# First score block in one plain fp32 pass, and what is rearranged around it

## Chip, cores, metric

The program runs on 1 core of a Trainium2 chip. The metric is device time in microseconds (us), the median of the runs. Lower is better.

## What is computed

Three parts follow each other: causal attention (2 batches, 12 heads, 448 positions, 64 per head), a token- and channel-mixing block, and a Fourier block with a normalized feed-forward network. Cut to the part that the change touches:

```python
scores = scale * np.matmul(q, k.transpose(0, 1, 3, 2))      # scale = 1 / 8
scores = np.where(mask, -1000000000.0, scores)              # mask: column > row
attn = np.exp(scores - np.max(scores, axis=-1, keepdims=True))
attn = attn / (np.sum(attn, axis=-1, keepdims=True) + 1e-09)
return np.matmul(attn, v)
```

Behind it stand `relu(xt @ w_tok1) @ w_tok2`, `relu(u @ w_ch1) @ w_ch2`, two Fourier transforms, and a feed-forward network with 3072 hidden channels.

## The kernel before

**Precision.** Products that must be exact to fp32 are split: an operand x becomes a rounded part "high" and a remainder "low", both of type fp32r, and the product is three fp32r passes: high x high, high x low, low x high. A plain fp32 matmul also exists in the kernel; the trace records each of those as two LDWEIGHTS and two MATMUL records. Transposes are single records.

**Pairs.** Attention goes by pairs of heads: 12 pairs (6 per batch). A pair's q and k lie as 128 x 448 tiles (64 rows for each head). `load_k` (K) loads k and q into staging slots, `k_high` (k) and `q_high` (q) round them on ScalarE (ACT), `k_low` (l, on GpSimd/POOL except for pair 0) and `q_low` (m, on VectorE/DVE) make the remainders. The four 112-row blocks of a pair's causal scores are made by `scores` (S) in three groups: S n.0 holds blocks 0 and 1, S n.1 block 2, S n.2 block 3. Block i needs 112 (i + 1) columns, but each pass has at least 256 columns (L336): `w = max(256, TS * (i + 1))`. The causal mask is added by bf16 matmuls (L354). Then follow the maxima (N, DVE), exps (E, ACT), transposes (T, L391, TensorE), their copies (C, DVE and ACT), the product with v (P, L408) and its copy (O, L416, ACT), the transposes of that (X, L427), the divisors (Z, L420) and the division (x, L440, DVE).

**Staging slots.** The loads of q and k use tiles that later hold the residual (they appear as `resid` in the trace). `stage(n)` (L290 to L292) hands them out in turn: six slots for pairs 0 to 4, three of them for pairs 5 to 11. A load into a slot waits until all readers of what was there are done. The order in which k and q of a pair take their slots is set in L297:

```python
c.k32, c.q32 = stage(n), stage(n)
nc.sync.dma_start(out=c.k32, in_=qk[b, hp, :, 1])
nc.sync.dma_start(out=c.q32, in_=qk[b, hp, :, 0])
```

So, from pair 6 on, k of pair n + 1 goes into the slot that q of pair n - 1 had, and q of pair n + 1 into that of k of pair n. All loads (q and k, v at L321, weights at L132) are issued by one queue, SP, in order.

**Order.** Every engine executes in the order of the program, and in the attention stage this order is written out by hand in the string `ORDER`: a letter, the pair and a part. The letters are those above, and R, W for loading and converting weights ahead (L132, L141 to L161), A, r, s, D, d for token mixing, B, b for channel layout, u, w for rounding the residual, h, g for rounding x. Within ORDER, `m8` (q_low of pair 8) stands behind `K9`, and `q10 u0.2 k10 R4 W4.0 N9.1 E9.0 O7 X7` is one stretch of line 84.

**Opening.** Before the attention stage TensorE executes seven 128 x 128 plain fp32 matmuls of a constant tile `mean_w` (L194), which VectorE has set (L117). POOL builds the identity and mask tiles (L267 to L276).

Of the kernel before, what the change touches and what calls it, by code (L numbers as in the profile page):

```python
# [10 lines left out]
F32 = mybir.dt.float32  # L11
# [59 lines left out]
ORDER = """K0 k0 l0 K1 q0 m0 S0.0 N0.0 N0.1 S0.1 N0.2 S0.2 k1 l1 N0.3 q1 m1 E0.0 E0.1 S1.0 N1.0 N1.1 K2 E0.2 S1.1 E0.3 T0.2 T0.0
N1.2 C0.2 k2 q2 E1.0 T0.1 T0.3 C0.0 T0.4 E1.1 l2 m2 S1.2 E1.2 S2.0 N1.3 V1 V0 C0.3 N2.0 C0.4 C0.1 P0 R0 W0.0 W0.1 N2.1
K3 K4 E1.3 k3 T1.0 T1.2 S2.1 T1.1 C1.0 O0 T1.4 T1.3 C1.2 X0 E2.0 q3 E2.1 N2.2 E2.2 S2.2 l3 m3 S3.0 C1.1 k4 Z0 x0 N2.3
C1.3 q4 C1.4 P1 N3.0 E2.3 T2.0 T2.3 T2.4 N3.1 S3.1 R1 W1.0 O1 T2.2 W0.2 m4 C2.0 B0.0 C2.3 T2.1 C2.4 X1 E3.0 E3.1 S3.2
N3.2 E3.2 l4 S4.0 V3 V2 b0.0 C2.1 C2.2 P2 W0.3 W0.4 W0.5 N3.3 N4.0 Z1 x1 N4.1 K5 q5 E3.3 T3.0 C3.0 T3.1 T3.2 Z2 O2
T3.4 k5 C3.2 C3.1 B0.1 X2 T3.3 E4.0 E4.1 S4.1 S4.2 C3.4 W1.1 b0.1 h0 C3.3 P3 l5 g0 N4.2 N4.3 E4.2 m5 S5.0 E4.3 S5.1 x2
T4.3 Z4 W1.2 Z3 T4.4 C4.4 O3 h1 T4.1 h2 T4.0 C4.3 T4.2 C4.0 C4.2 N5.0 X3 K6 C4.1 k6 N5.2 N5.1 B0.2 g2 g1 R2 W2.0 q6
A0.1 A0.0 x3 V5 V4 W1.3 W2.1 E5.0 E5.1 S5.2 l6 m6 E5.2 S6.0 W1.4 K7 r0.0 N5.3 P4 E5.3 S6.1 N6.0 N6.1 s0.0 r0.1 b0.2
T5.4 O4 k7 s0.1 X4 T5.1 T5.0 C5.4 T5.2 E6.0 E6.1 x4 W1.5 D0.0 C5.1 D0.1 N6.2 C5.0 T5.3 W2.2 S6.2 E6.2 q7 h3 l7 m7 S7.0
d0.1 C5.2 K8 q8 C5.3 P5 N6.3 R3 k8 h4 N7.0 E6.3 N7.1 d0.0 T6.4 T6.2 T6.0 E7.0 E7.1 S7.1 S7.2 O5 T6.3 l8 g4 V6 K9 C6.3  # L80
k9 C6.2 C6.4 B1.1 X5 C6.0 T6.1 D0.2 N7.2 m8 q9 Z5 x5 N7.3 W2.3 b1.1 B1.2 C6.1 B1.0 P6 Z6 d0.2 E7.2 S8.0 N8.0 N8.1 h5
E7.3 T7.3 O6 b1.2 T7.0 b1.0 T7.2 C7.3 T7.4 T7.1 C7.0 X6 E8.0 E8.1 S8.1 S8.2 C7.1 W2.4 Z7 g5 g3 C7.2 A1.1 C7.4 A1.0 x6
N8.2 B2.0 N8.3 W3.0 W3.1 W3.2 E8.2 l9 m9 S9.0 E8.3 S9.1 V7 P7 V8 K10 r1.1 s1.1 u0.1 h6 W2.5 Z8 u0.0 r1.0 s1.0 N9.0
T8.0 W3.3 T8.1 b2.0 T8.3 q10 u0.2 k10 R4 W4.0 N9.1 E9.0 O7 X7 C8.1 C8.0 T8.4 E9.1 C8.3 D1.0 x7 B2.1 T8.2 N9.2 S9.2 m10
E9.2 l10 w0.1 S10.0 C8.4 d1.0 C8.2 P8 b2.1 N9.3 E9.3 T9.2 T9.1 D1.1 W3.4 O8 h7 K11 q11 T9.0 W4.1 N10.0 N10.1 W4.2 C9.2
T9.3 C9.1 T9.4 E10.0 C9.3 E10.1 d1.1 X8 C9.0 D1.2 S10.1 S10.2 m11 x8 h8 k11 C9.4 V9 P9 V11 Z9 u1.0 N10.2 E10.2 N10.3
E10.3 d1.2 O9 W3.5 l11 S11.0 S11.1 B2.2 R5 W5.0 b2.2 T10.1 C10.1 T10.0 T10.2 g7 g8 w0.2 w0.0 g6 N11.0 N11.2 N11.1
T10.3 C10.3 u1.2 E11.0 A2.0 r2.0 C10.2 C10.0 X9 T10.4 W4.3 A2.1 W5.1 x9 W5.2 W4.4 E11.1 S11.2 s2.0 V10 C10.4 P10 N11.3
u1.1 E11.2 r2.1 s2.1 E11.3 T11.2 C11.2 T11.0 C11.0 T11.1 O10 T11.4 T11.3 W5.3 C11.4 X10 W4.5 R6 W6.0 W6.1 Z10 R7 C11.1
C11.3 P11 w1.2 D2.0 O11 X11 x10 D2.2 d2.2 Z11 x11 h10 d2.0 B3.1 b3.1 u2.0 h9 W5.4 w1.1 w1.0 U0 g10 B3.2 U1 W6.2 u2.2  # L90
y0 b3.2 h11 B3.0 y1 W5.5 W7.0 W7.1 W6.3 W6.4 g9 g11 A3.0 A3.1 z0 D2.1 b3.0 r3.0 s3.0 W7.2 z1 W7.3 r3.1 s3.1 U2 y2 D3.0
D3.1 d3.0 z2 d3.1 W7.4 U3 D3.2 y3 u3.1 W6.5 W7.5 w2.2 w2.0 d2.1 u3.0 u2.1 w3.0 w3.1 w2.1 z3 Y0 a0 d3.2 Y1 a1 u3.2 w3.2
"""


# [5 lines left out]
def fused_kernel(ctx: ExitStack, tc: tile.TileContext, qk, v, w1, w2, wa, wb, wc, wd, fa, fb, out):  # L101
    nc = tc.nc
# [12 lines left out]
    make_identity(nc, ident)  # L115
    mean_w = const.tile([128, 128], F32, name="mean_w")
    vec.memset(mean_w, 1.0 / DM)  # L117
    ones = const.tile([1, 128], F32, name="ones")
    vec.memset(ones, 1.0)
    eps_t = const.tile([128, 16], F32, name="eps_t")[:, :1]  # L120
    vec.memset(eps_t, EPS)
# [68 lines left out]

    ps = ctx.enter_context(tc.tile_pool(name="ps", bufs=1, space=bass.MemoryType.PSUM))
    psum = ps.tile([128, 8, 512], F32, name="psum")
    for _ in range(7):
        mm(psum[:, 7, :128], lhsT=mean_w, rhs=mean_w, start=True, stop=True)  # L194
    turn = dict(y=0, s=0, all=0)

    def take(ring, n):
# [63 lines left out]
    with ExitStack() as actx:  # L261
# [28 lines left out]
        def stage(n):  # L290
            staged[0] += 1
            return resid[staged[0] % 6 if n < 5 else 3 + staged[0] % 3][1]  # L292

        def load_k(n):
            c = pairs[n]
            b, hp = n // 6, n % 6
            c.k32, c.q32 = stage(n), stage(n)  # L297
            nc.sync.dma_start(out=c.k32, in_=qk[b, hp, :, 1])
            nc.sync.dma_start(out=c.q32, in_=qk[b, hp, :, 0])

# [709 lines left out]
```

## Time and profile before

| | |
|---|---|
| median of 3 runs | 685.57 us (685.55 to 686.62) |
| profiled execution, span from first to last instruction | 687.0 us |
| TensorE (PE) busy | 680.4 us, 99% |
| VectorE (DVE) busy | 534.8 us, 78% |
| ScalarE (ACT) busy | 291.7 us, 42% |
| GpSimd (POOL) busy | 125.5 us, 18% |
| q and k loads | 24, 224 KB each, 3.2 us from issue to landing (median) |

The profiled execution is one run more; its own time is the span. A busy share is an average over stages: the attention stage takes the first 125 us, in which ACT and DVE are busier than on average. TensorE's records overlap and their ends are modelled, so the distance between starts is what a matmul costs. An idle time in brackets at the end of a timeline row is what the engine stood still before that row, with what released it.

### The profile page before, as it was taken

What the parts mean: (1) busy time and instruction counts of PE and PEld (TensorE: products, weight loads), DVE (VectorE), ACT (ScalarE), POOL (GpSimd) and SP (SyncE); (2) the same over time, 40 slices, a digit from 0 to 9 for tenths busy, and PEclk for the clock granted to TensorE, in tenths of its full rate; (3) what the DMA queues carried; (4) which work ended last, traced back from release to release, by engine and by line L of the source; (5) the groups of instructions that cost most, each with busy time, mean ns of one, the idle gap of its engine ahead of it and who ended that gap; (6) DMA issues with size and microseconds to landing.
All of it is one profiled execution on the core that took longest, in us unless ns stands there. A gap on an engine that the chain in (4) does not pass through costs nothing.

```text
span 687.0 us, 10288 instructions
## 1 busy us (share of the span) xinstructions
PE 680.4 (99%) x3946; PEld 623.8 (91%) x3946; DVE 534.8 (78%) x885; ACT 291.7 (42%) x624; POOL 125.5 (18%) x106
## 2 busy tenths in 40 slices
PE   8999999999999999999999999999999999999997
PEld 7778888999999999999999999999999999999997
DVE  5997887367987975799989987989887898655851
ACT  6988987433333323244455522223443233323200
POOL 3153327420000000130140004372003221000000
PEclk9999999999999999999999999999999999999999
DMA  8234221164344342200223342324232434222311
GB/s 268 68 103 138 91 99 45 49 234 151 125 127 133 111 149 95 93 1 1 92 77 108 123 144 76 120 92 153 93 122 93 155 124 151 93 84 83 108 48 54
DMA packets 20577, 73.38 MB, mean 107 GB/s; under 512 B 2334, under 2 KB 6942, under 8 KB 20160
## 3 DMA queue, kind: packets, MB, share of 16 engines
q1 hardware_dynamic: 19952, 69.48, 30.7%
q0 software_dynamic: 576, 3.25, 1.4%
q8 instruction: 31, 0.51, 0.3%
q14 instruction: 18, 0.15, 0.1%
HBM read 69.96 MB, written 2.75 MB: 106 GB/s over the span
## 4 chain that ended last, share of the span: by engine, by line
PE 98%; DVE 1%; DMA 0%; ACT 0%; issue 0%; DVEq 0%
PE psum L247 13%; PE psum L226 13%; PE psum L227 13%; PE psum L252 13%; PE psum L251 13%; PE psum L228 12%; PE psum L340 4%; PE psum L391 4%; PE psum L408 3%; PE psum L472 2%; PE psum L503 2%; PE psum L701 2%; PE psum L770 1%; PE psum L354 1%; PE psum L427 1%; PE psum L490 1%
## 5 line engine op out<-in xcount | busy, mean ns | idle before, releaser
L247 PE MATMUL psum<-gh,wh 128*128 128x448 f32 x432 | 157.4, 364 | 0.0
L226 PE MATMUL psum<-acth,wh 128*128 128x448 f32 x432 | 156.9, 363 | 0.0
L252 PE MATMUL psum<-gl,wh 128*128 128x448 f32 x432 | 156.5, 362 | 0.0
L227 PE MATMUL psum<-acth,wl 128*128 128x448 f32 x432 | 156.4, 362 | 0.0
L251 PE MATMUL psum<-gh,wl 128*128 128x448 f32 x432 | 156.1, 361 | 0.0
L228 PE MATMUL psum<-actl,wh 128*128 128x448 f32 x432 | 155.9, 361 | 0.0
L141 ACT ACTIVATE m<-w 128x512 f32<-128x512 f32 (+2 forms) x92 | 71.0, 773 | 127.4 <-DVE wl L161 83.0
L159 ACT CAST wh<-m 128x512 fp32r<-128x512 f32 (+1 forms) x90 | 63.4, 705 | 91.6 <-PE psum L252 52.1
L252 PEld LDWEIGHTS psum<-gl,wh 128*128 128x128 f32 x432 | 81.0, 188 | 6.4 <-DVE gl L234 0.4
L226 PEld LDWEIGHTS psum<-acth,wh 128*128 128x128 f32 x432 | 81.1, 188 | 5.7
L228 PEld LDWEIGHTS psum<-actl,wh 128*128 128x128 f32 x432 | 80.9, 187 | 5.8
L251 PEld LDWEIGHTS psum<-gh,wl 128*128 128x128 f32 x432 | 80.9, 187 | 5.5 <-issue 0.2
L247 PEld LDWEIGHTS psum<-gh,wh 128*128 128x128 f32 x432 | 81.1, 188 | 5.2 <-issue 0.2
L227 PEld LDWEIGHTS psum<-acth,wl 128*128 128x128 f32 x432 | 81.0, 188 | 4.6
L161 DVE TENSOR_TENSOR wl<-m,wh 128x512 fp32r<-128x512 f32 (+1 forms) x84 | 69.5, 830 | 14.3 <-ACT wh L159 13.9
L143 DVE TENSOR_SCALAR m<-m 128x512 f32<-128x512 f32 (+2 forms) x92 | 49.9, 543 | 38.8 <-ACT m L141 38.3
L148 DVE SCALAR_TENSOR_TENSOR m<-w,m 128x512 uint32<-128x512 uint32 (+2 forms) x92 | 78.5, 853 | 2.1
L152 DVE SCALAR_TENSOR_TENSOR m<-w,m 128x512 uint32<-128x512 uint32 (+2 forms) x92 | 78.2, 850 | 2.0
L232 ACT ACTIVATE gh<-psum 128x448 fp32r<-128x448 f32 x72 | 37.7, 540 | 65.0 <-PE psum L228 64.8
L234 DVE SCALAR_TENSOR_TENSOR gl<-psum,gh 128x448 fp32r<-128x448 f32 x72 | 43.8, 619 | 26.0 <-ACT gh L232 26.0
L378 ACT ACTIVATE p<-psum,nmx 112x112 f32<-112x112 f32 (+3 forms) x96 | 46.5, 503 | 10.6 <-DVE nmx L363 9.4
L144 DVE TENSOR_SCALAR m<-m 128x512 uint32<-128x512 uint32 (+2 forms) x92 | 48.0, 522 | 2.4
(158 smaller groups left out, 838.0 us busy)
## 6 DMA issues: line engine op xcount, KB each, us to landing
w<-in_wc SPq DMA_DIRECT2D x24, 768.0 KB, 4.3
w<-in_wd SPq DMA_DIRECT2D x36, 512.0 KB, 3.4
w<-in_wa SPq DMA_DIRECT2D x12, 768.0 KB, 4.3
w<-in_wb SPq DMA_DIRECT2D x18, 512.0 KB, 3.4
resid<-in_qk SPq DMA_DIRECT2D x24, 224.0 KB, 3.2
v<-in_v SPq DMA_DIRECT2D x12, 224.0 KB, 2.9
out<-t SPq DMA_DIRECT2D x12, 224.0 KB, 1.9
w<-in_w SPq DMA_DIRECT2D x2, 896.0 KB, 7.5
```

The costliest lines, as they stand in the source:

```text
L141: act.activation(out=m, in_=hi.bitcast(F32), func=AF.Abs)
L143: vec.tensor_scalar(out=m, in0=m, scalar1=F64_MIN, scalar2=F64_MAX, op0=ALU.max, op1=ALU.min)
L148: vec.scalar_tensor_tensor(out=mu, in0=lo, scalar=29, in1=mu, op0=ALU.logical_shift_right, op1=ALU.bitwise_or)
L152: vec.scalar_tensor_tensor(out=mu, in0=hi, scalar=0xC0000000, in1=mu, op0=ALU.bitwise_and, op1=ALU.bitwise_or)
L159: act.copy(wh, m)
L161: low_engine[0].tensor_tensor(out=wl, in0=m, in1=f(wh), op=ALU.subtract)
L226: mm(pb[:, :S], lhsT=lh, rhs=act_h[ct][b], start=ct == 0, stop=False)
L227: mm(pb[:, :S], lhsT=ll, rhs=act_h[ct][b], start=False, stop=False)
L228: tail[0] = mm(pb[:, :S], lhsT=lh, rhs=act_l[ct][b], start=False, stop=ct == NCT - 1).ins
L247: mm(pb[:, :S], lhsT=lh, rhs=gh, start=j + k == 0 and seeded is None, stop=False, skip_group_check=seeded is not None,)
L251: mm(pb[:, :S], lhsT=ll, rhs=gh, start=False, stop=False, skip_group_check=seeded is not None)
L252: tail[0] = mm(pb[:, :S], lhsT=lh, rhs=gl, start=False, stop=j == last and k == nk - 1, skip_group_check=seeded is not None,).ins
```

## The change

1. Block 0 of every pair is one plain fp32 matmul per head over 112 columns: k as loaded, times a new tile q0 (the first 112 columns of q, scaled by 1/8). `q_first` (letter e) makes q0 on POOL; the tile has one buffer. e stands behind q of the same pair in ORDER.
2. k as loaded is now read by S n.0 too. q and k of a pair take their slots in the other order, while the k load is still issued first; so k of pair n + 1 goes into the slot of q of pair n, and q of pair n + 1 into that of k of pair n - 1. In ORDER, m8 moves ahead of K9. Nothing else in ORDER moves.
3. The opening matmuls take a broadcast constant 1.0, which the program's own preamble sets, in place of `mean_w`.
4. `divisors` adds 1e-9 by a scalar_tensor_tensor, with a maximum against the sum itself, in place of a tensor_scalar.
5. The tile `ones` shrinks from 128 to 16 columns; some bookkeeping (`hasattr`, a dict for `raw`) has no instruction.

```diff
@@ ORDER (core of it)
-K0 k0 l0 K1 q0 m0 S0.0 N0.0 N0.1 S0.1 N0.2 S0.2 k1 l1 N0.3 q1 m1 E0.0
+K0 k0 l0 K1 q0 e0 m0 S0.0 N0.0 N0.1 S0.1 N0.2 S0.2 k1 l1 N0.3 q1 e1 m1 E0.0
...
-S7.2 O5 T6.3 l8 g4 V6 K9 C6.3 k9 C6.2 C6.4 B1.1 X5 C6.0 T6.1 D0.2 N7.2 m8 q9 Z5
+S7.2 O5 T6.3 l8 g4 V6 m8 K9 C6.3 k9 C6.2 C6.4 B1.1 X5 C6.0 T6.1 D0.2 N7.2 q9 e9 Z5
...
-    ones = const.tile([1, 128], F32, name="ones")
+    ones = const.tile([1, 16], F32, name="ones")
...
+    warm = nc.const_aps.tensor(1.0, [128, 128], F32)
     for _ in range(7):
-        mm(psum[:, 7, :128], lhsT=mean_w, rhs=mean_w, start=True, stop=True)
+        mm(psum[:, 7, :128], lhsT=warm, rhs=warm, start=True, stop=True)
...
-            c.k32, c.q32 = stage(n), stage(n)
+            c.q32, c.k32 = stage(n), stage(n)
...
+        def q_first(n):
+            c = pairs[n]
+            c.q0 = a1.tile([128, TS], F32, tag="q0", name="q0")
+            pool.tensor_scalar(out=c.q0, in0=c.q32[:, :TS], scalar1=0.125, scalar2=None, op0=ALU.mult)
...
-                w = max(256, TS * (i + 1))
-                for m, (qt, kt) in enumerate(((c.qh, c.kh), (c.qh, c.kl), (c.ql, c.kh))):
+                w = TS if i == 0 else max(256, TS * (i + 1))
+                passes = ((c.q0, c.k32),) if i == 0 else ((c.qh, c.kh), (c.qh, c.kl), (c.ql, c.kh))
+                for m, (qt, kt) in enumerate(passes):
...
-            vec.tensor_scalar(out=c.ssum, in0=c.ssum, scalar1=1.0e-9, scalar2=None, op0=ALU.add)
+            vec.scalar_tensor_tensor(out=c.ssum, in0=c.ssum, scalar=1.0e-9, in1=c.ssum, op0=ALU.add, op1=ALU.max)
```

## Rows read from the trace of the kernel before

**Rows 1.** The chain that ended last, whole span: shares by engine.
```profile
PE 98%; DVE 1%; DMA 0%; ACT 0%; issue 0%; DVEq 0%
```
**Rows 2.** Timeline of TensorE, pair 5, block 1: start, duration (us), line, tiles.
```profile
44.72 0.28 PE L340 MATMUL psum<-kh,qh 64*112 64x256 f32 x2
...
44.95 0.28 PE L340 MATMUL psum<-kh,ql 64*112 64x256 f32 x2
```
**Rows 3.** Timeline of TensorE: product with v, then transposes (followed at 30.03).
```profile
26.70 2.11 PE L408 MATMUL psum<-pt,v 112*64 112x448 f32 x16
28.74 1.36 PE L391 MATMUL psum<-ident,p 112*112 112x112 f32 x12
```
**Rows 4.** Timeline of the opening, all engines.
```profile
3.88 0.39 POOL L276 TENSOR_SCALAR_AFFINE_SELECT maskb<-maskb 56x224 bf16<-56x224 bf16 x1
...
4.67 0.61 DVE L317 SCALAR_TENSOR_TENSOR ql<-resid,qh 128x448 fp32r<-128x448 f32 x1
...
6.33 0.57 PE L354 MATMUL psum<-maskb,identb 56*112 56x224 bf16 x4
...
11.11 0.56 PE L340 MATMUL psum<-kh,ql 64*112 64x256 f32 x2 [0.65 <-DVE ql L317]
...
12.10 0.58 PE L354 MATMUL psum<-maskb,identb 56*112 56x224 bf16 x4
...
13.64 3.90 PE L391 MATMUL psum<-ident,p 112*112 112x112 f32 x20
```
**Rows 5.** Timeline of POOL and VectorE: two overlaps of the one with the other.
```profile
34.89 2.37 POOL L161 TENSOR_TENSOR w1l<-m,w1h 112x1024 fp32r<-112x1024 f32 x1 [7.20 <-ACT w1h L159]
...
35.01 2.27 DVE L420 TENSOR_SCALAR ssum<-ssum 112x8 f32<-112x8 f32 x1
...
420.72 2.62 POOL L898 TENSOR_TENSOR resid<-resid,mu 128x448 f32<-128x448 f32 x2
...
422.25 1.64 DVE L152 SCALAR_TENSOR_TENSOR m<-w,m 128x512 uint32<-128x512 uint32 x1
```
**Rows 6.** ql of pairs 7 and 9; a weight load's issue; landings of q, of weights.
```profile
62.05 0.63 DVE L317 SCALAR_TENSOR_TENSOR ql<-resid,qh 128x448 fp32r<-128x448 f32 x1 [0.29 <-ACT qh L313]
...
84.01 0.62 DVE L317 SCALAR_TENSOR_TENSOR ql<-resid,qh 128x448 fp32r<-128x448 f32 x1
...
78.39 0.38 SPq L132 DMA_DIRECT2D w<-in_wa  x1
...
DMA to landing us min/median/max: 2.5/2.9/7.9
...
DMA to landing us min/median/max: 4.3/4.9/5.3
```
**Rows 7.** Timeline of ScalarE at pairs 5, 8 and 10.
```profile
34.68 0.60 ACT L313 ACTIVATE qh<-resid 128x448 fp32r<-128x448 f32 x1
...
35.77 0.66 ACT L378 ACTIVATE p<-psum,nmx 112x448 f32<-112x448 f32 x1
...
63.42 0.58 ACT L313 ACTIVATE qh<-resid 128x448 fp32r<-128x448 f32 x1 [0.89 <-PE psum L340]
...
65.93 0.63 ACT L378 ACTIVATE p<-psum,nmx 112x448 f32<-112x448 f32 x1
...
87.30 0.94 ACT L141 ACTIVATE m<-w 128x768 f32<-128x768 f32 x1
...
88.83 0.53 ACT L416 COPY ots<-psum 128x448 f32<-128x448 f32 x1
```
**Rows 8.** Timeline of TensorE at pair 4's scores and at three runs of transposes.
```profile
33.28 0.35 PE L340 MATMUL psum<-kh,qh 64*112 64x256 f32 x2
...
38.30 0.98 PE L391 MATMUL psum<-ident,p 112*112 112x112 f32 x8 [0.93 <-DVE x L440]
...
66.56 1.36 PE L391 MATMUL psum<-ident,p 112*112 112x112 f32 x12
...
89.91 0.60 PE L427 MATMUL psum<-ident,ots 128*112 128x128 f32 x4
```

More of the change, by code (lines that the diff above doesn't have):

```diff
@@ L68 @@
 ENGINES = {getattr(mybir.EngineType, e) for e in ("PE", "DVE", "Activation", "Pool", "SP")}
[L71 to L89, printed above, removed]
@@ L90 @@
-C11.3 P11 w1.2 D2.0 O11 X11 x10 D2.2 d2.2 Z11 x11 h10 d2.0 B3.1 b3.1 u2.0 h9 W5.4 w1.1 w1.0 U0 g10 B3.2 U1 W6.2 u2.2
-y0 b3.2 h11 B3.0 y1 W5.5 W7.0 W7.1 W6.3 W6.4 g9 g11 A3.0 A3.1 z0 D2.1 b3.0 r3.0 s3.0 W7.2 z1 W7.3 r3.1 s3.1 U2 y2 D3.0
-D3.1 d3.0 z2 d3.1 W7.4 U3 D3.2 y3 u3.1 W6.5 W7.5 w2.2 w2.0 d2.1 u3.0 u2.1 w3.0 w3.1 w2.1 z3 Y0 a0 d3.2 Y1 a1 u3.2 w3.2
+ORDER = """K0 k0 l0 K1 q0 e0 m0 S0.0 N0.0 N0.1 S0.1 N0.2 S0.2 k1 l1 N0.3 q1 e1 m1 E0.0 E0.1 S1.0 N1.0 N1.1
+K2 E0.2 S1.1 E0.3 T0.2 T0.0 N1.2 C0.2 k2 q2 e2 E1.0 T0.1 T0.3 C0.0 T0.4 E1.1 l2 m2 S1.2 E1.2 S2.0 N1.3 V1 V0
@@ new lines @@
+C0.3 N2.0 C0.4 C0.1 P0 R0 W0.0 W0.1 N2.1 K3 K4 E1.3 k3 T1.0 T1.2 S2.1 T1.1 C1.0 O0 T1.4 T1.3 C1.2 X0 E2.0 q3
+e3 E2.1 N2.2 E2.2 S2.2 l3 m3 S3.0 C1.1 k4 Z0 x0 N2.3 C1.3 q4 e4 C1.4 P1 N3.0 E2.3 T2.0 T2.3 T2.4 N3.1 S3.1
+R1 W1.0 O1 T2.2 W0.2 m4 C2.0 B0.0 C2.3 T2.1 C2.4 X1 E3.0 E3.1 S3.2 N3.2 E3.2 l4 S4.0 V3 V2 b0.0 C2.1 C2.2 P2
+W0.3 W0.4 W0.5 N3.3 N4.0 Z1 x1 N4.1 K5 q5 e5 E3.3 T3.0 C3.0 T3.1 T3.2 Z2 O2 T3.4 k5 C3.2 C3.1 B0.1 X2 T3.3
+E4.0 E4.1 S4.1 S4.2 C3.4 W1.1 b0.1 h0 C3.3 P3 l5 g0 N4.2 N4.3 E4.2 m5 S5.0 E4.3 S5.1 x2 T4.3 Z4 W1.2 Z3 T4.4
@@ new lines @@
+C4.4 O3 h1 T4.1 h2 T4.0 C4.3 T4.2 C4.0 C4.2 N5.0 X3 K6 C4.1 k6 N5.2 N5.1 B0.2 g2 g1 R2 W2.0 q6 e6 A0.1 A0.0
+x3 V5 V4 W1.3 W2.1 E5.0 E5.1 S5.2 l6 m6 E5.2 S6.0 W1.4 K7 r0.0 N5.3 P4 E5.3 S6.1 N6.0 N6.1 s0.0 r0.1 b0.2
+T5.4 O4 k7 s0.1 X4 T5.1 T5.0 C5.4 T5.2 E6.0 E6.1 x4 W1.5 D0.0 C5.1 D0.1 N6.2 C5.0 T5.3 W2.2 S6.2 E6.2 q7 e7
+h3 l7 m7 S7.0 d0.1 C5.2 K8 q8 e8 C5.3 P5 N6.3 R3 k8 h4 N7.0 E6.3 N7.1 d0.0 T6.4 T6.2 T6.0 E7.0 E7.1 S7.1
+S7.2 O5 T6.3 l8 g4 V6 m8 K9 C6.3 k9 C6.2 C6.4 B1.1 X5 C6.0 T6.1 D0.2 N7.2 q9 e9 Z5 x5 N7.3 W2.3 b1.1 B1.2
@@ new lines @@
+C6.1 B1.0 P6 Z6 d0.2 E7.2 S8.0 N8.0 N8.1 h5 E7.3 T7.3 O6 b1.2 T7.0 b1.0 T7.2 C7.3 T7.4 T7.1 C7.0 X6 E8.0
+E8.1 S8.1 S8.2 C7.1 W2.4 Z7 g5 g3 C7.2 A1.1 C7.4 A1.0 x6 N8.2 B2.0 N8.3 W3.0 W3.1 W3.2 E8.2 l9 m9 S9.0 E8.3
+S9.1 V7 P7 V8 K10 r1.1 s1.1 u0.1 h6 W2.5 Z8 u0.0 r1.0 s1.0 N9.0 T8.0 W3.3 T8.1 b2.0 T8.3 q10 e10 u0.2 k10 R4
+W4.0 N9.1 E9.0 O7 X7 C8.1 C8.0 T8.4 E9.1 C8.3 D1.0 x7 B2.1 T8.2 N9.2 S9.2 m10 E9.2 l10 w0.1 S10.0 C8.4 d1.0
+C8.2 P8 b2.1 N9.3 E9.3 T9.2 T9.1 D1.1 W3.4 O8 h7 K11 q11 e11 T9.0 W4.1 N10.0 N10.1 W4.2 C9.2 T9.3 C9.1 T9.4
@@ new lines @@
+E10.0 C9.3 E10.1 d1.1 X8 C9.0 D1.2 S10.1 S10.2 m11 x8 h8 k11 C9.4 V9 P9 V11 Z9 u1.0 N10.2 E10.2 N10.3 E10.3
+d1.2 O9 W3.5 l11 S11.0 S11.1 B2.2 R5 W5.0 b2.2 T10.1 C10.1 T10.0 T10.2 g7 g8 w0.2 w0.0 g6 N11.0 N11.2 N11.1
+T10.3 C10.3 u1.2 E11.0 A2.0 r2.0 C10.2 C10.0 X9 T10.4 W4.3 A2.1 W5.1 x9 W5.2 W4.4 E11.1 S11.2 s2.0 V10 C10.4
+P10 N11.3 u1.1 E11.2 r2.1 s2.1 E11.3 T11.2 C11.2 T11.0 C11.0 T11.1 O10 T11.4 T11.3 W5.3 C11.4 X10 W4.5 R6
+W6.0 W6.1 Z10 R7 C11.1 C11.3 P11 w1.2 D2.0 O11 X11 x10 D2.2 d2.2 Z11 x11 h10 d2.0 B3.1 b3.1 u2.0 h9 W5.4
@@ L93 @@
+w1.1 w1.0 U0 g10 B3.2 U1 W6.2 u2.2 y0 b3.2 h11 B3.0 y1 W5.5 W7.0 W7.1 W6.3 W6.4 g9 g11 A3.0 A3.1 z0 D2.1
+b3.0 r3.0 s3.0 W7.2 z1 W7.3 r3.1 s3.1 U2 y2 D3.0 D3.1 d3.0 z2 d3.1 W7.4 U3 D3.2 y3 u3.1 W6.5 W7.5 w2.2 w2.0
+d2.1 u3.0 u2.1 w3.0 w3.1 w2.1 z3 Y0 a0 d3.2 Y1 a1 u3.2 w3.2
 """
@@ L327, in scores @@
             c = pairs[n]
-            if g == 0:
+            if not hasattr(c, "sp"):
                 c.sp, c.se = {}, {}
@@ L357, in maxima @@
             c = pairs[n]
-            if i == 0:
+            if not hasattr(c, "nmx"):
                 c.nmx = small(ap, "nmx")
@@ L371, in exps @@
             c = pairs[n]
-            if i == 0:
+            if not hasattr(c, "p"):
                 c.ssum = small(tiny, "ssum")
@@ L519, in fused_kernel @@
         sources += [(wb[0, ct, 0], None, None) for ct in EARLY_DOWN]
-        raw, ahead, g0 = [], [None] * (len(sources) - 2), {}
+        raw, ahead, g0 = {}, [None] * (len(sources) - 2), {}
         def load_raw(k):
-            raw.append(fetch(sources[k][0]))
+            raw[k] = fetch(sources[k][0])
         steps = {}
@@ L547, in fused_kernel @@
         ops = dict(
-            K=load_k, k=k_high, l=k_low, q=q_high, m=q_low, V=load_v, S=scores, N=maxima, E=exps, T=transposes,
+            K=load_k, k=k_high, l=k_low, e=q_first, q=q_high, m=q_low, V=load_v, S=scores, N=maxima, E=exps, T=transposes,
             C=pt_copy, P=pv, O=pv_copy, Z=divisors, X=rows, x=divide, h=x_high, g=x_low, A=mix_in, r=mix_high,
```

## The prediction

> **What bounds the kernel now.** I read four views, in this order. The chain that ended last comes first: TensorE holds 98% of it [rows 1], so only what shortens TensorE's stream, or makes it wait, moves the time. Next, the timeline of TensorE in the attention stage (the first 125 us of 687.0), where all edits lie. It shows what the edited matmuls cost: one pass over 256 columns for both heads takes 0.115 us, as the first and the third pass of block 1 start 0.23 us apart, and blocks 0 and 1 are runs of three such passes [rows 2]. Two heads run side by side, in the two halves of the rows. Third, the timelines of the opening 14 us [rows 4], where TensorE still waits for others. Last, the load queue with the Vector and Scalar instructions that open or use its slots [rows 6, 7], because the change exchanges the slots in which q and k land. The reader should see there that one in-order queue issues the q and k loads as slots fall free, and when Scalar reads what they bring.
>
> **Block 0 in plain fp32.** Removed: three passes of 256 columns for each of 12 pairs, 3 x 0.115 = 0.35 us a pair. Added: one plain fp32 matmul of 112 columns for each head, which the trace records twice, as it does every plain fp32 matmul. No plain fp32 matmul on half the rows is in the trace. The nearest row is the product with v, two heads on half the columns each: 16 records of 448, 336, 224 and 112 columns take 2.04 us from 26.70 to 28.74 [rows 3]. That is 4480 columns at 0.455 ns; four records of 112 columns by that rate are 0.20 us. The far end is the transposes: twelve of 112 columns in 1.29 us (28.74 to 30.03), 0.107 us each, bound by loading 112 columns of weights or by streaming; four in turn would be 0.43 us. I take 0.20, since heads side by side is what both score and v rows show, so 0.15 us is saved a pair, 1.5 us over pairs 2 to 11. The ends are 0.20 and 0.43, that is 1.5 us gained to 0.8 us lost.
>
> **The opening.** The seven opening matmuls need no Vector memset any more and would start and end a little earlier. Nothing waits for their end, so this is costed at nothing: the cover is the wait for the first scores' operands, and the cost without that cover is still no more than their present place. The first score block now needs q0 from POOL. POOL's set-up ends at 3.88 + 0.39 = 4.27 [rows 4]. The new operation reads 112 elements of one operand; a POOL select of 224 half-size elements takes 0.39 [rows 4], so 0.2 to 0.4, and I take 0.3. It must also share with Vector, which is busy with kl0 and then, from 4.67 to 5.28, ql0. The rows show the sharing: an 8-element Vector operation took 2.27 us at 35.01, ending as POOL's 2.37 us subtraction from 34.89 ended, and a Vector scalar_tensor_tensor that began at 422.25 ended only 0.55 us after POOL's of 420.72 to 423.34 [rows 5]. So I put the operation between kl0 and ql0: q0 at about 5.0, the block by 5.5, block 1's passes by 6.2, where the masks stood at 6.33 [rows 4]: 0.1 us. Pair 1 gains more. There the pass with ql stands at 11.11, waiting for Vector, and the masks follow four passes later, at 12.10; now one pass follows instead of four, and the masks come at about 11.3: 0.8 us. This stretch runs at half the rate: 20 transposes take 3.90 us from 13.64, 0.195 each against 0.107 later [rows 3, 4]; the lower level is 1.2 GHz. A lead of 0.8 us there is worth half of it once the rate doubles: 0.4 us (0 to 1.2).
>
> **The divisor edit.** It replaces the 8-element tensor_scalar by a scalar_tensor_tensor with two SBUF operands. Without a collision both cost the same. With one, the row at 422.25 is of just such an instruction and it waited for POOL, so I leave the 2.1 us of that wait where it is [rows 5]. Were it gone, x would come up to 2.1 us earlier and TensorE's wait of 0.93 us for it at 38.30 [rows 8] would go, unless the exps that it transposes are late. The Trainium skill, "SBUF — State Buffer", section "Who interferes with whom", tells of an exclusive lock of a port pair, which Vector takes for a tensor_scalar in a fast mode and also, against a POOL instruction that reads SBUF, for any instruction with two SBUF inputs; the rows agree with both, and by that rule the new form gains nothing and the sum stays as it is.
>
> **The loads.** Today k of pair n+1 takes the slot of q of pair n-1. After the change k of pair n+1 takes the slot of q of pair n, and is issued only when ql of pair n has been written; q of pair n+1 stands behind it in the queue. A load lands 2.5 to 2.9 us after its issue (the 7.9 belongs to the crowded opening), a weight load of 768 KB 4.3 to 5.3 [rows 6]; I take 2.7 and 4.9. An issue takes 0.38 us. Three places are short of time:
> - Pair 5 (its k takes the slot of pair 4's k, now also read by pair 4's block 0, at 33.28 to 33.55 [rows 8]): k's load at 33.6, q's at 34.0, landing at 36.7, where Scalar reads it at 34.68 [rows 7]. Scalar is 2.0 us late with pair 3's last exps, the second of which ended at 36.4 [rows 7]. The eight transposes ahead of 38.30 need them and end near 38.9; as TensorE waits until 38.30 anyway [rows 8], 0.6 us is lost (0 to 1.2).
> - Pair 8: ql of pair 7 is written at 62.05 to 62.68 [rows 6]; k's load follows at 62.7, q's at 63.1, landing at 65.8, where Scalar reads it at 63.42 [rows 7]. Behind that read on Scalar stand a copy for the product of pair 5, k's rounding and pair 6's exps, the last of which began at 65.93. It feeds the transposes of 66.56 [rows 8] from their third on, so there is 0.2 us of slack: 2.4 - 0.2 = 2.2 us lost (2.0 to 2.9).
> - Pair 10: ql of pair 9 is written at 84.01 to 84.63 [rows 6]. Three loads follow: k, q, and the weight load that today goes out at 78.39. It now goes at about 85.5 and lands at 90.4. Scalar converts it at 87.30 [rows 7]: 3.1 us late, and with it the copy at 88.83 that ends at 89.36. TensorE's transposes of that copy start at 89.91 [rows 8], so 3.1 - 0.6 = 2.5 us lost (1.9 to 2.9).
>
> Pairs 6, 7, 9 and 11 are late at issue too, but their q and k are read several us after that; pair 9 is helped by its own edit, which moves ql of pair 8 into a stretch where Vector waits. The value loads behind these are used much later; the weight load behind pair 6's is late too, and its cover is a run of 24 token-mixing matmuls that need nothing new from Scalar. POOL's twelve small operations, 12 x 0.3 us, lie in its idle time (it waits for Scalar before nearly every one of its own).
>
> **Sum.** -1.5 - 0.4 + 0.6 + 2.2 + 2.5 = +3.4 us. Against the profiled span of 687.0 that is 690.4. The runs' median, 685.57, lies 1.4 us below that span, so I forecast 689.0 us.
>
> **Rivals.** *The waits are covered.* Scalar has gaps in this stage; if what stands behind the late reads is needed later than I read it, nothing is lost. It decides at pair 8: TensorE keeps its pace if q lands by about 63.6, so if ql of pair 7 is written 2.2 us earlier than now; the same holds at pair 10. The time is then 685.6 - 1.9 = 683.7, and 682.8 if the divisor edit also frees the 0.93 us. For it: Scalar stands idle for 0.89 us ahead of that read even now [rows 7]. Against: what ends this is TensorE itself, and ql of pair 7 waits for Scalar [rows 6], so it can't come much earlier. *Only one of the two long waits reaches TensorE:* 685.6 + 0.9 to 1.2, about 686.6. *The two heads run in turn:* the block then costs 0.43 instead of 0.35, and 1.5 us gained becomes 0.8 lost: 691.3. *The clock rises earlier:* fewer waits between 5 and 12 us may let TensorE reach 2.4 GHz ahead of the 20 transposes that now take 3.90 us; they would take 2.1, and the sum falls by 1.8 to 687.2. The Trainium skill, "TensorE: Matmul & The Clock Gate", Part 1, says that activity releases the throttled clock; the rows show only that it rose during or after those transposes [rows 4].
>
> **How the numbers follow.** Forecast 0.43, one wait only 0.17, covered 0.22, in turn 0.08, clock 0.10. A measurement of this kernel can tell 0.2%, 1.4 us, from no change: under 684.2 is faster, over 686.9 slower. Covered is faster: 0.22. One wait, and a part of the clock's case, is the same: 0.20. The rest is slower: 0.58. The range reaches from beyond the covered case, 683.2, to 690.8, which takes in the forecast with most of its bounds; the forecast's own range is 687.2 to 690.8.
>
> **What would show it.** Right: the new score matmuls, two records a head, take 0.2 us a pair; Scalar waits for a load ahead of L313 near 64 and ahead of L141 near 87; TensorE has new waits of about 2 us at the transposes after each. Wrong: Scalar's waits there are under 1 us, or TensorE stays without waits while Scalar has them. If the 2.27 us at 35 is gone, I misjudged the divisor edit.

## The result and the profile after

The changed kernel takes 694.65 us (median of 4 runs, 693.78 to 696.24) against 685.56 us: 1.0133 of the time before, 95% interval 1.0117 to 1.0149. That is 9.1 us slower, where 3.4 were forecast. Its profiled execution has a span of 692.2 us and took 693.93 us. A difference of 1.7 to 1.9 us between a run's time and its span is there in every run, so a span is not the run's own time. The first profiled execution of before, 687.0 us of span, was therefore one of some 688.7 us and about 3 us longer than the usual run of 685.6. A second profile of before (experiment 1) has a span of 684.5, and differences below are taken against that one.

The chain of waits, which was 98% TensorE [rows 1], now leaves TensorE. Its shares by engine, from the page of the kernel after:

```profile
PE 93%; ACT 2%; DMA 2%; DVE 1%; issue 1%; POOL 1%; SPq 0%; POOLq 0%; ACTq 0%; DVEq 0%
```

What TensorE waits for, whole span of the kernel after (total in us, times, longest):

```profile
PE psum L437 <- ACT ots L426: 3.8, 1, 3.8
PE psum L350 <- ACT p L388: 2.0, 2, 1.8
PE psum L350 <- POOL q L326: 1.0, 1, 1.0
PE psum L418 <- ACT pt L410: 1.0, 1, 1.0
```

(L437 transposes `ots`, L350 are the scores, L418 is the product with v.) The third row and 1.8 us of the second are in the opening; POOL's q there is the new tile q0, which the trace calls q. The first and the last are new, at pairs 10 and 8. Their place on ScalarE, with pair 6's (timeline of the kernel after; the first row's releaser was long done, and run 4's trace names the weight tile there; in brackets the idle time before and who ended it); these answer to [rows 7]:

```profile
46.55 0.92 ACT L144 ACTIVATE m<-w 128x768 f32<-128x768 f32 x1 [2.47 <-POOL kl L312]
...
62.46 0.58 ACT L317 ACTIVATE qh<-resid 128x448 fp32r<-128x448 f32 x1 [3.33 <-DMA resid<-in_qk]
...
86.66 0.58 ACT L317 ACTIVATE qh<-resid 128x448 fp32r<-128x448 f32 x1 [1.91 <-DMA resid<-in_qk]
...
90.44 0.89 ACT L144 ACTIVATE m<-w 128x768 f32<-128x768 f32 x1 [2.28 <-DMA w<-in_wa]
...
91.89 0.53 ACT L426 COPY ots<-psum 128x448 f32<-128x448 f32 x1
```

The load queue of the kernel after explains all four (L302 is k's load, L303 q's, L135 a weight tile's). At each place k's load waits until VectorE has written the ql of the pair before, and q and the weight tile stand behind it. First the queue's own wait for ql between 20 and 100 us (total in us, times, longest), then its timeline:

```profile
SPq L302 <- DVE ql L321: 47.7, 7, 11.0
```

```profile
40.09 0.33 SPq L302 DMA_DIRECT2D resid<-in_qk  x1
40.52 1.16 SPq L303 DMA_DIRECT2D resid<-in_qk  x1
41.73 0.44 SPq L135 DMA_DIRECT2D w<-in_wa  x1
...
59.34 0.33 SPq L302 DMA_DIRECT2D resid<-in_qk  x1
59.76 0.38 SPq L303 DMA_DIRECT2D resid<-in_qk  x1
...
83.50 0.35 SPq L302 DMA_DIRECT2D resid<-in_qk  x1
83.90 0.42 SPq L303 DMA_DIRECT2D resid<-in_qk  x1
84.37 0.43 SPq L135 DMA_DIRECT2D w<-in_wa  x1
```

The chain of waits of the kernel after, in order of time, runs through the last of these loads:

```profile
84.37 5.99 DMA w<-in_wa
...
90.44 0.04 ACT m L144
...
91.23 0.77 ACT p L388 x4
92.00 0.43 ACT ots L426
...
92.47 0.54 PE psum L437 x3
```

TensorE after this wait, against 89.91 in [rows 8], and the stretches around it (us, busy time and instructions of each engine, then the granted clock):

```profile
87.27 1.36 PE L401 MATMUL psum<-ident,p 112*112 112x112 f32 x12
92.47 0.65 PE L437 MATMUL psum<-ident,ots 128*112 128x128 f32 x4 [3.84 <-ACT ots L426]
```

```profile
10.00:15.00 5.00, 4.94 (x41) 4.61 (x37) 3.47 (x6) 5.00 (x21) 1.63 (x2) 0.66 1.02 262
...
90.00:95.00 5.00, 2.53 (x13) 2.36 (x14) 1.77 (x3) 3.99 (x13) 0.45 (x1) 0.83 0.00 0
95.00:100.00 5.00, 5.00 (x43) 3.73 (x43) 3.85 (x7) 2.16 (x8) 1.48 (x1) 0.82 0.44 138
```

The granted clock is 0.83 and 0.82 of full speed there. As the clock has two levels, 1.2 and 2.4 GHz, that is (0.17 + 0.18) x 2 x 5 = 3.5 us at the lower one. It fell once more between 10 and 15 us.

What went as forecast: block 0, four records of 112 columns, takes 0.22 us from its start to that of block 1, where 0.20 was forecast (timeline of TensorE after, pair 5; `resid` is k as loaded, q is q0; against 0.35 for three passes, by [rows 2]):

```profile
40.19 0.45 PE L350 MATMUL psum<-resid,q 64*112 64x112 f32 x4
40.41 0.35 PE L350 MATMUL psum<-kh,qh 64*112 64x256 f32 x2
```

Not as forecast: the divisors of pair 1, 2.27 us in [rows 5], take 0.16. Here they begin ahead of POOL's subtraction (timelines of VectorE and of POOL, after):

```profile
32.42 0.16 DVE L430 SCALAR_TENSOR_TENSOR ssum<-ssum 112x8 f32<-112x8 f32 x1
```

```profile
32.53 2.38 POOL L164 TENSOR_TENSOR w1l<-m,w1h 112x1024 fp32r<-112x1024 f32 x1 [7.04 <-ACT w1h L162]
```

**Where the time goes.** Worked out from the traces: TensorE's runs of matmuls are matched in order, and the start in the second trace of before is taken from the start in the other trace (us; the head row is the time in before).

```
                          15     36     45     62     82     88    100    125    300    680
after                  +0.19  -1.65  -1.87  -1.20  +1.08  +4.97  +6.62  +6.48  +7.71  +7.70
2  mean_w              -0.37  -2.23  -2.44  +0.79  +3.13  +7.19  +8.85  +8.72  +9.83  +9.83
3  q8 first            -0.41  -2.28  -2.49  -1.73  -0.79  +3.81  +4.92  +4.79  +5.62  +5.62
4  ql of pair 9 early  -0.37  -2.23  -2.45  -1.42  +2.18  +2.02  +2.06  +1.91  +2.74  +2.74
5  R4 early            -0.53  -2.37  -2.59  -1.40  +0.99  +2.48  +2.53  +2.37  +3.17  +3.17
6  R4 and q10 early    -0.37  -2.24  -2.45  +2.61  +5.00  +4.91  +4.96  +4.81  +6.24  +6.23
8  three moves         -1.57  -3.09  -3.27  -3.63  -2.76  -2.92  -3.09  -3.25  -2.62  -2.63
9  four slots          -0.53  -2.38  -2.59  -2.92  -3.07  -3.23  -3.19  -3.34  -2.54  -2.55
12 before, R4 late     -1.44  -1.10  -1.10  -1.10  -1.10  +3.65  +4.28  +4.28  +4.66  +4.66
```

The changed kernel gains 1.8 us between 15 and 36 us, then loses 0.7 at pair 6 (45 to 62), 2.3 at pair 8 (62 to 82), 3.9 at pair 10 (82 to 88), 1.65 at the lower clock (88 to 100) and 1.2 later. That is 7.7 in the profiled executions. The runs differ by 9.1: after's profiled execution lies 0.7 us below the median of its runs, as two of the four are longer than it by 1.5 and 2.3 us, and the second profiled execution of before lies 0.7 us above before's median. No trace of the longer runs exists. But pair 6 (45 to 62 us), whose loads are those of after in runs 2 to 6 as well, costs 0.8 to 1.2 us in the traces of runs 3, 4 and 5, and 3.2 and 5.1 in those of runs 2 and 6, where the clock falls behind the wait. So its price is not the same in every execution.

### The profile page after: what moved, and what is told of

Same layout as the page of the kernel before. It is cut to its first block, busy times and chain, and to the rows that moved or that the text cites. A ratio compares the mean times of both kernels' runs of the same rounds, so it can differ in the third digit from the quotient of the medians.

```text
span 692.2 us, 10275 instructions
## 1 busy us (share of the span) xinstructions
PE 679.0 (98%) x3922; PEld 620.9 (90%) x3922; DVE 533.3 (77%) x885; ACT 291.2 (42%) x624; POOL 132.5 (19%) x118
## 4 chain that ended last, share of the span: by engine, by line
PE 93%; ACT 2%; DMA 2%; DVE 1%; issue 1%; POOL 1%; SPq 0%; POOLq 0%; ACTq 0%; DVEq 0%
PE psum L231 13%; PE psum L251 12%; PE psum L256 12%; PE psum L230 12%; PE psum L255 12%; PE psum L232 12%; PE psum L401 3%; PE psum L418 3%; PE psum L350 3%; PE psum L513 2%; PE psum L482 2%; PE psum L711 2%; DMA w<-in_wa 2%; PE psum L780 1%; ACT p L388 1%; PE psum L500 1%
```

## Experiments

**1. Before, once more.**

> The kernel before, unchanged, profiled once more. The trace of before has a span of 687.0 us, above every timed run of it but one, and rows in its opening at half rate (20 transposes from 13.64 take 3.90 us); the trace of after has them at half rate only for 3.4 us and stands 2.5 us ahead by then. Theory A (the 2.5 us come from the change's opening): this trace looks like the first one, clock rising near 17 us, span 687 again, and runs of 685.6. Theory B (when the clock rises in the opening differs from execution to execution, whatever the kernel): the transposes at 13.6 us take about 2.1 us or the rise comes at another time, and the span is 683 to 685, 2 to 3 us shorter than the first trace.

685.9 us (10 runs, 685.53 to 687.05), 1.0003 of before (0.9994 to 1.0013); span 684.5. The same 20 transposes that took 3.90 us from 13.64 [rows 4] start at 12.50 here and run at twice the rate (timeline of TensorE):

```profile
12.50 1.75 PE L391 MATMUL psum<-ident,p 112*112 112x112 f32 x16
```

Theory B: when the clock rises in the opening differs between executions of the same program. The 2.5 us that after seems to gain at 15 us against the first trace are not the change's: against this trace it is 0.2 us behind.

**2. The old opening operand in the changed kernel.**

```diff
-    warm = nc.const_aps.tensor(1.0, [128, 128], F32)
+    warm = mean_w
```

> The kernel after, with the opening matmuls reading mean_w again; all else as after. Theory A (the operand set up earliest lets TensorE's clock rise sooner): the seven matmuls start at 1.05 us instead of 0.76, the clock rises later than 4.7 us, and the kernel is 1.5 to 2.5 us slower than after's 694.65. Theory B (chance of the execution, or the shorter block 0): it stands within 0.7 us of after, and its marks at 20 us are no later than after's by more than 0.3 us.

697.25 us, with runs from 693.93 (mean granted clock 0.998) to 699.68 (0.989). The median looks like Theory A, but the trace stands 0.56 us ahead of after's at 15 us, so the opening is no slower. What is longer is a fall of the clock near 51 us, behind a wait of 1.2 us at pair 6, which after's trace lacks. By itself inconclusive on the operand; runs 10 and 11 bound it.

**3. Pair 8's q ahead of its k.**

```diff
-            nc.sync.dma_start(out=c.k32, in_=qk[b, hp, :, 1])
-            nc.sync.dma_start(out=c.q32, in_=qk[b, hp, :, 0])
+            pair = (c.q32, 0), (c.k32, 1)
+            for t, x in pair if n == 8 else pair[::-1]:
+                nc.sync.dma_start(out=t, in_=qk[b, hp, :, x])
```

> The kernel after, with pair 8's q load issued ahead of its k load; q's slot has been free long since, only k's slot waits for ql of pair 7. Theory A (pair 8's q is late only because its load stands behind k's in the queue): Scalar's wait for q8 near 60 us goes, TensorE's 1.0 us wait ahead of the product with v near 63 us goes, and 2.0 to 2.4 us are gained, 692.4. Rival (the extra work on POOL's in-order queue, e and the low part of x, or k8 itself, is what is late): under 0.5 us gained, and the wait moves to kh of pair 8.

692.31 us, 2.3 less than after, as Theory A had it, but in part by luck: of the 2.1 us between the two traces, pair 8 gives 1.3 and the opening 0.6. And the rival's wait is there as well: ScalarE now waits 0.96 us for k8 at 61.45, and between 62 and 82 us 0.9 us are still lost (table above). So q's lateness accounts for some 1.3 us of the 2.3 that after loses in that stretch and, as run 9 loses nothing there, k's for the rest.

**4. ql of pair 9 earlier.**

```diff
-... q9 e9 Z5 x5 N7.3 ... W3.2 E8.2 l9 m9 S9.0 ...
+... q9 e9 m9 Z5 x5 N7.3 ... W3.2 E8.2 l9 S9.0 ...
```

> The kernel after, with ql of pair 9 written right behind q0 of pair 9 in the order, as the change did for pair 8; three loads of pair 10 (k, q and the weight tile behind them) then go out about 8 us earlier. Theory A (the late issue of these three loads costs the 3.8 us ahead of the transposes of ots at 92.5 us, and the stand of TensorE there is what lowers the clock for 3.4 us): both go, 3.9 us of wait and 1.5 us of half clock, so 5.0 to 5.6 us faster than after, about 689.3. Rival (the clock falls there for another reason, as it did at 11.5 us): only 3.5 to 4 us gained, and 3.4 us at the lower level stay somewhere near 90 us.

689.02 us, 5.6 less than after. The wait of 3.8 us and the lower clock near 93 us are gone together: between 82 and 100 us the trace loses nothing. The new place has a price of its own: pair 8's stretch (62 to 82 us) loses 3.6 us here, 2.3 in after. TensorE waits 1.0 us at 72.20, ahead of transposes of x. The profile names exps for this wait, but in ORDER those stand behind the transposes; what these need is pair 5's division (x5), and in VectorE's queue it now stands behind m9, which waited 1.48 us for its operand:

```profile
70.31 0.63 DVE L319 SCALAR_TENSOR_TENSOR ql<-resid,qh 128x448 fp32r<-128x448 f32 x1 [1.48 <-ACT qh L315]
...
71.36 0.69 DVE L448 TENSOR_TENSOR x<-psum,ssum 112x512 f32<-112x512 f32 x1
```

**5 and 6. The weight load ahead of pair 10's loads; and pair 10's q ahead of its k as well.**

```diff
-... S9.1 V7 P7 V8 K10 ... q10 e10 u0.2 k10 R4 W4.0 ...
+... S9.1 V7 P7 V8 R4 K10 ... q10 e10 u0.2 k10 W4.0 ...
```

Run 6 has beside this the diff of run 3 with `n == 10`.

> The kernel after, with the fifth weight load (R4) issued ahead of pair 10's k and q loads instead of behind them; the loads of k and q still wait for ql of pair 9. Theory A (the weight tile is what is late last: Scalar waits 1.91 us for q10 and then 2.28 us more for this tile): Scalar's second wait goes, TensorE's 3.8 us at the transposes of ots become about 1.6, so 2.2 us are gained, 692.4, and 1.5 more if the clock no longer falls there. Rival (q10 alone sets it): nothing gained, under 0.5 us.

> As the run with the weight load early, and pair 10's q load ahead of its k load, so that neither waits for ql of pair 9; only k10 does, which Scalar reads last. Theory A (q10 accounts for 1.9 us of Scalar's lateness, the weight tile for 2.3): TensorE's wait at the transposes of ots is under 0.7 us, no half clock near 93 us, 5 us faster than after, 689.6. Rival (k10, still late, takes the place of q10 on Scalar): 1 us or more of wait stays there, with kh of pair 10 as what Scalar waits for.

Run 5: 689.3 us, 5.3 less than after, where Theory A had 2.2, or 3.7 with the clock. The traces differ by 4.5: 2.4 between 82 and 88 us, 1.6 of clock, the rest elsewhere. ScalarE (timeline) still waits 1.89 us for q10, and the weight tile is there when its turn comes:

```profile
86.54 0.58 ACT L315 ACTIVATE qh<-resid 128x448 fp32r<-128x448 f32 x1 [1.89 <-DMA resid<-in_qk]
...
87.94 0.91 ACT L142 ACTIVATE m<-w 128x768 f32<-128x768 f32 x1
```

TensorE's wait there (waits of TensorE, 85 to 95 us) falls from 3.8 to 1.5 us, by the 2.3 us of ScalarE's second wait, and the clock doesn't fall behind it:

```profile
PE psum L435 <- ACT ots L424: 1.5, 1, 1.5
```

Run 6: 688.47 us (687.96 to 692.45), 1.1 under Theory A's 689.6. TensorE has no wait at the transposes of ots; ScalarE waits only 0.29 us for k10. Its profiled execution was the slowest of its six: a wait of 1.7 us at pair 6, and then a granted clock (windows) of

```profile
50.00:55.00 5.00, 5.00 (x28) 3.31 (x30) 2.54 (x5) 4.34 (x14) 2.57 (x2) 0.53 0.30 92
55.00:60.00 5.00, 5.00 (x44) 3.78 (x40) 1.83 (x5) 3.01 (x13) 1.15 (x1) 0.78 0.01 3
```

So both loads are late at pair 10 and each has its share: 1.5 us the q, 2.3 the weight tile behind it.

**7. The new divisors alone, in the kernel before.**

```diff
-            vec.tensor_scalar(out=c.ssum, in0=c.ssum, scalar1=1.0e-9, scalar2=None, op0=ALU.add)
+            vec.scalar_tensor_tensor(out=c.ssum, in0=c.ssum, scalar=1.0e-9, in1=c.ssum, op0=ALU.add, op1=ALU.max)
```

> The kernel before, with the new form of the divisors alone (scalar_tensor_tensor with two operands in place of tensor_scalar). In both traces of before the divisors of pair 1 begin 0.11 to 0.12 us after POOL's subtraction into w1l and take 2.27 and 2.32 us; in the trace of after they begin 0.11 us before it and take 0.16. Theory A (the form makes no difference, as I predicted; only the moment did): the instruction takes 2.2 us or more again, TensorE still waits some 0.95 us for x at 36 us, and the time is that of before, 685.6. Rival (the new form isn't held up by POOL): it takes 0.2 us, TensorE's wait goes, 0.9 us faster, 684.7.

685.65 us, 0.9998 of before (0.9987 to 1.0008). The new form is held up just as the old one was (VectorE, POOL, and a wait of TensorE, in this run):

```profile
31.52 2.30 DVE L420 SCALAR_TENSOR_TENSOR ssum<-ssum 112x8 f32<-112x8 f32 x1
```

```profile
31.41 2.39 POOL L161 TENSOR_TENSOR w1l<-m,w1h 112x1024 fp32r<-112x1024 f32 x1 [7.21 <-ACT w1h L159]
```

```profile
PE psum L391 <- DVE x L440: 0.9, 1, 0.9
```

Theory A. In all five traces of the old program (two of before, runs 7, 10 and 12) the divisors begin 0.10 to 0.12 us behind POOL's instruction and take 2.3 us, in either form; in all nine of the changed kernels they begin 0.09 to 0.17 us ahead of it and take 0.16, with POOL's own 2.4 unchanged. The Trainium skill, "SBUF — State Buffer", section "Who interferes with whom", says that issue order, and not the shape of the operation, decides who blocks; these traces agree.

**8. Three moves.** Beside run 3's diff:

```diff
-... X3 K6 C4.1 k6 N5.2 N5.1 B0.2 g2 g1 R2 W2.0 q6 ...
+... X3 R2 K6 C4.1 k6 N5.2 N5.1 B0.2 g2 g1 W2.0 q6 ...
-... P6 Z6 d0.2 E7.2 S8.0 ... E8.2 l9 m9 S9.0 ...
+... P6 Z6 d0.2 m9 E7.2 S8.0 ... E8.2 l9 S9.0 ...
```

> The kernel after with three moves: pair 8's q load ahead of its k load; ql of pair 9 written some 9 us earlier, in a stretch where Vector waits (so that pair 10's three loads go out earlier); the third weight load (R2) ahead of pair 6's k and q instead of behind them. Theory A (the loss is made of late issues on the one load queue, at pairs 6, 8 and 10, and of nothing else): all TensorE waits of after that hang on them go, no half clock after 20 us, and what is left is the gain of the shorter block 0 and of the divisors, 684.3, that is 1 to 1.5 us faster than before. Rival (the small q0 operations on POOL, or k's own late landing, cost something of their own): 686 or more, with a wait for kh, kl or xl in its place.

684.71 us (10 runs, 683.6 to 685.4), 0.9982 of before (0.997 to 0.9993): 0.2% faster than before, near Theory A's 684.3. R2 goes out at 29.78 instead of 41.73, and the loss at pair 6 becomes a gain of 0.36 between 45 and 62 us. 0.87 us are still lost at pair 8, where k8 is late, as in run 3.

**9. Four slots, ORDER untouched.**

```diff
-            return resid[staged[0] % 6 if n < 5 else 3 + staged[0] % 3][1]
+            if n < 5:
+                return resid[staged[0] % 6][1]
+            return resid[(3 if n == 11 else 0, 3, 4, 5)[staged[0] % 4]][1]
```

> The kernel after with its ORDER untouched, but four slots instead of three for q and k of pairs 5 to 10 (a residual tile that nothing uses until later); pair 11 as in after. No load then waits for ql of the pair before. Theory A (the exchange of slots, by which k of pair n+1 waits for ql of pair n, with q and a weight tile behind it, is the whole loss): the waits at pairs 6, 8 and 10 all go without any other edit, 684.3 to 685.0, as in the run with the three moves. Rival (m8's move, the POOL operations or the order itself cost something): 686.5 or more.

683.94 us (10 runs, 683.08 to 684.25), 0.9968 of before (0.9958 to 0.9978): the fastest. Its loads of pairs 6, 8 and 10 go out at 30.64, 49.79 (q8) and 70.42, the weight tiles right behind (load queue):

```profile
30.64 0.33 SPq L304 DMA_DIRECT2D resid<-in_qk  x1
31.06 0.38 SPq L305 DMA_DIRECT2D resid<-in_qk  x1
31.50 0.42 SPq L135 DMA_DIRECT2D w<-in_wa  x1
...
70.42 0.36 SPq L304 DMA_DIRECT2D resid<-in_qk  x1
70.87 0.38 SPq L305 DMA_DIRECT2D resid<-in_qk  x1
71.34 0.38 SPq L135 DMA_DIRECT2D w<-in_wa  x1
```

TensorE has no named wait at all behind 15 us, and of the queue's waits for ql one is left between 20 and 100 us, that of pair 11:

```profile
SPq L304 <- DVE ql L323: 15.3, 1, 15.3
```

One slot more takes 10.7 us off the changed kernel's 694.65. So the loads that wait for the ql of the pair before were the loss; m8's move and POOL's twelve small operations (0.49 us in the median, not 0.3), both still in, cost nothing that this run shows. No run has the new block 0 with three slots in the old order, so whether the exchange was needed is not shown.

**10 and 11. The opening operand alone in before, and mean_w in the kernel of run 8.** The diff of 10 is that of run 2 reversed.

> The kernel before with the opening matmuls reading the constant 1.0 that is set up earliest; nothing else. So far the clock rose at 17.3, 10.1 and 4.2 us in three traces with mean_w and block 0 in three passes, and at 4.6, 9.1, 9.8, 3.8, 9.4 and 4.3 us with the constant. Theory A (the operand moves only work that nothing waits for): 685.6, within 0.4 us of before. Rival (the 0.3 us earlier start lets the clock rise sooner): 0.5 to 1.5 us faster than before, rise at or under 5 us.

> The kernel with the three moves (684.71), its opening matmuls reading mean_w again. Theory A (no effect of the operand): 684.7, within 0.4. Rival: 0.5 to 1.5 us slower.

686.25 us, 1.0002 of before (0.9993 to 1.0011); and 684.86 us, 0.9982 of before (0.9972 to 0.9992), where run 8 has 0.9982. The medians are 0.5 us above that of before in the same series (685.74) and 0.15 above run 8's; by the intervals, these runs could tell some 0.7 us. The operand makes no difference of that size.

**12. The wait alone, in the kernel before.**

```diff
-... N7.3 W2.3 b1.1 ... C7.1 W2.4 Z7 ... h6 W2.5 Z8 ... N9.0 T8.0 ... k10 R4 W4.0 ...
+... N7.3 b1.1 ... C7.1 Z7 ... h6 Z8 ... N9.0 W2.3 T8.0 ... k10 W2.4 W2.5 R4 W4.0 ...
```

> The kernel before, none of the change in it; only the weight load R4 is held back, because its buffer is freed about 9 us later (the last three conversion steps of the third weight tile are moved behind the maxima of pair 9). Theory A (a stand of TensorE of about 4 us at the transposes of ots is what lowers the clock behind it): TensorE waits 3.5 to 5 us there, the clock is at its lower level for 3.4 us right behind, and the time is before's plus the wait plus 1.5 us, some 691. Rival (the lower clock near 93 us belongs to the new program, not to the wait): the wait alone, some 689.6, and the granted clock stays at 1.0 there.

692.21 us, by the medians 6.5 more than before (ratio 1.0087, 1.0069 to 1.0105), a little over Theory A's 691. The wait, and the clock over the next 5 us (timeline, then windows):

```profile
90.43 1.10 PE L428 MATMUL psum<-ident,ots 128*112 128x128 f32 x4 [3.82 <-ACT ots L417]
```

```profile
90.00:95.00 5.00, 4.57 (x24) 4.21 (x26) 3.28 (x6) 3.77 (x12) 0.00 (x0) 0.67 0.10 37
95.00:100.00 5.00, 5.00 (x53) 3.72 (x52) 4.62 (x8) 3.05 (x9) 0.91 (x1) 1.00 0.07 10
```

A late weight tile in the old program gives the same wait and a fall of the clock with it. The lower clock is a price of the wait, not of the change.

## Why the prediction was wrong

The direction and the mechanism held: pairs 8 and 10 are late for the reason given, on the queue named. At pair 10 the wait is where the prediction put it. At pair 8 the way was another: forecast were about 2 us at the transposes, and TensorE lost 1.8 us at the product with v (a named wait of 1.0), which needs the copy behind q8 on ScalarE, and 0.7 at the transposes. That 2.2 was right there is in part luck. The sum failed, by the size of pair 10 and by three terms put at nothing. Its terms beside what the traces show; a measured price is after's change over the stretch less that of run 9, which has the same edits without the late loads:

| term | forecast | shown | from |
|---|---|---|---|
| block 0, a pair | -0.15 | -0.15 to -0.17 | run 9: 0.33 over pairs 6 and 7, 0.15 from 100 to 125 us |
| opening | -0.4 | +0.2, within chance | after at 15 us, its own fall of the clock included |
| divisors of pair 1 | 0 | -1.0 | wait of 0.96 us gone |
| pair 5 | +0.6 | 0 | after and run 9 alike from 36 to 45 us |
| pair 6 | 0 | +1.0 | +0.67 against -0.33 |
| pair 8 | +2.2 | +2.4 | +2.28 against -0.15 |
| pair 10 | +2.5 | +4.1 | +3.89 against -0.16 |
| lower clock behind pair 10 | none | +1.6 | +1.65 against +0.04 |
| behind 125 us | none | +1.2 | see below |

**Pair 10 is the term that was mis-sized.** "It now goes at about 85.5 and lands at 90.4": the issue came when it should (84.37, with TensorE some 1.3 us further along than in the first trace), but the load took 5.99 us, not the 4.9 of a usual one. The rows behind the 4.9 have one load of 224 KB right ahead of them, not two. Here k and q, 448 KB, went out in the 0.9 us before it. So it is with another weight load of after (6.1 us) and three of run 9 (6.4 to 6.5), while in run 5, sent 9 us ahead of k and q, this load took 4.2. That they share the transfer engines is how I read it. The issues of the kernel after between 83 and 91 us (KB each, median us from issue to landing):

```profile
w<-in_wa SPq DMA_DIRECT2D x1, 768.0 KB, 6.0
resid<-in_qk SPq DMA_DIRECT2D x2, 224.0 KB, 2.7
```

**The clock was no term at all.** I counted a wait of TensorE at its own length. A wait of 3.8 to 4.0 us at this place was followed by the lower level in all four traces that have it (after, runs 2, 3 and 12), and cost 1.6 to 1.7 us more than the wait; in the six with 1.5 us or none there (4, 5, 6, 8, 9 and 11) nothing followed. The falls near 51 us, in the traces of runs 2 and 6, came behind waits of 1.2 and 1.7 us at pair 6, so the length of the wait alone doesn't tell.

**Pair 6's cover was too short.** The weight load there is late, "and its cover is a run of 24 token-mixing matmuls that need nothing new from Scalar". The matmuls need nothing, but the exps behind the late conversion do reach TensorE: ScalarE stood 2.47 us ahead of it, of which 1.0 came through.

**Pair 5 was a slot read wrongly.** Of pair 5 I wrote that "its k takes the slot of pair 4's k"; it takes that of pair 4's q. It waits for ql of pair 4 only, goes out at 27.57, and nothing is late.

**The divisor edit.** The reading of its form was right and run 7 shows it. But "I leave the 2.1 us of that wait where it is" was wrong: the wait hung on 0.12 us of order between two engines, and the changed kernel turned it. Which of its edits did so stays open: run 7 clears the form alone, run 10 the opening's operand. The shorter blocks ahead are my guess.

**The opening.** The 0.4 us were worked out for a first trace in which the clock rose late. The rival "the clock rises earlier" described that trace's chance and no effect of the edit. At 15 us the traces of changed kernels stand from 1.6 us ahead to 0.2 behind (table above), those of the old program from 1.4 ahead to 2.5 behind; an effect of 0.4 can't be read from them. And setting the runs' median 1.4 us below the span compared one run with others as if it were usual; a run's time lies 1.7 to 1.9 us above its span. The forecast didn't suffer: 685.6 + 3.4 is 689.0 too.

**Behind 125 us** after loses 0.6 us around 150 us, 0.3 of it a named wait for gl (the remainder of a hidden activation behind the attention stage; run 12, an old program, loses 0.4 there too), and another 0.6 between 160 and 300 us in small steps. All nine traces of kernels with the change show these 0.6 us, and none of the five of the old program. No wait is named at these steps. What causes them stays open.

**The rivals.** The covered case was to give 683.7 and to hold if pair 8's q landed by about 63.6. In run 9 its load goes out at 49.79, and the time is 683.94. But run 9 is also free of the divisors' wait, for which that rival had 682.8; that it came out by the other figure is in part luck, as 0.8 us went behind 125 us. Heads in turn is out, by the 0.22 us of block 0, and one wait only is out, as both reach TensorE.

## What to carry to other kernels

An edit by which a load waits for a later reader of its buffer is paid for on the load queue: list every transfer that stands behind the one that now waits, and follow each to the engine that reads it. The weight tile, third in the queue, cost more here than the q load itself. A stand of the matmul engine can cost more than its length; here 3.8 to 4.0 us brought 3.4 us at half rate each time. And before a profile is compared with another, see that its own time agrees with the runs. Here the first trace's opening carried 2.5 us that belonged to no edit.

## What was not expected of the hardware

The clock of TensorE rose in the opening at different times in executions of one and the same program: 20 transposes took 3.90 us in the first trace of before, and 16 of them 1.75 us in the second, from 12.50. Which chip ran the program doesn't settle it: on each of two chips the clock rose near 4 us in some traces and near 9 us in others, though of different programs. In after's opening it had risen already and fell again: 0.66 between 10 and 15 us, where TensorE had stood for 1.8 us shortly before. And an eight-element VectorE instruction took 0.16 us where it began 0.11 us ahead of POOL's subtraction, and 2.3 us where it began as much behind it.
